# A written-out order of two blocks in turn, with one gating product in six moved from VectorE to GpSimd

## The chip, the cores and the metric

The kernel runs on one core of a Trainium2 chip. The metric is the device time of one execution in microseconds (us). Before the change the median of three runs is 351.76 us (350.42 to 352.13). A smaller time is better. Engines are named as in the profile: PE (TensorE), with PEld for its weight loads, DVE (VectorE), ACT (ScalarE), POOL (GpSimd) and SP (SyncE, which only issues transfers here).

## The reference

Two layers follow each other. The first is a causal convolution over 7 tokens with softmaxed weights per head (8 heads of 24 channels). The second multiplies a value projection by a gate and projects the product; the gate is the sigmoid of a causal per-channel convolution over 5 tokens.

```python
w = softmax(weight)                                    # (8 heads, 7 taps)
out = einsum('hk,bskhg->bshg', w, windows_of_7(x))     # x: (8, 4224, 192)
gate_pre = sum(conv_w[k] * shifted(out, k) for k in range(5))
gate = 1 / (1 + exp(-gate_pre))
val = out @ w_val                                      # 192 x 192
return (gate * val) @ w_out                            # 192 x 192
```

## The kernel before

Channels lie on partitions and tokens along the free axis. The 192 channels of a token are cut in two: 128 channels fill all partitions, and the other 64 of two halves of the batch lie above each other. So a block of m tokens (482 in most blocks, 432 and 288 in the first ones) has three parts: chunk 1, two columns groups of 128 x m (written 128x964 in the profile), and chunk 2, one of 128 x m (128x482). There are 37 blocks (0 to 36), which come from 14 groups of input; a group of the long kind holds three blocks.

For each group PE makes the first convolution as many small products with a banded matrix (`conv_unit`, L323), in units of up to 7 windows; two units belong to each block. ACT copies each half of a unit out of its bank to SBUF (`evict`, L335, tile `e`), and transfers (L381) bring it into the layout of the blocks. The five-token gate convolution is then built on DVE in two PSUM accumulators: `pa` for chunk 1 and `pb` for chunk 2. ACT opens an accumulator with the first tap (L418), DVE adds the four others (L436, a "tap"; A below stands for a tap of `pa`, B for one of `pb`), and ACT closes it with the sigmoid (L449, tile `g`).

The value projection `v` and the output projection `o` are done in split precision. An operand is cast to a rounded high part (`xh` for the input, `ph` for the gated product) and a low part, the difference (`xl`, `pl`, POOL, L458 for chunk 1 and L466 for chunk 2); three products high x high, low weight x high, high x low are summed. The cast of chunk 1 is ACT's (L457), that of `xh` of chunk 2 POOL's in most blocks and that of `ph` of chunk 2 ACT's (both L465). On PE one block has these stages: `diagonal` (L492, 64x64 products), `columns` (L540, 128x64), `rows` (L529, 64x128) and `main` (L507, 128x128), for v of block n and o of block n-1. Gating is DVE's: `gated` multiplies the bank of v by `g` in place (L558), once for chunk 2 and twice for chunk 1. ACT copies the three banks of o to SBUF (`project`, L574), and SP sends them out. In the last seven blocks chunk 2 of v is first copied from its bank by ACT (L746, tile `vt`) and multiplied on POOL (L750).

The order on every engine is the order in which the program calls these functions; a loop body from L705 on is the same for blocks 4 to 29. Five PSUM banks are handed out in rotation to v, o and the units, whichever comes next; each taker waits for whoever reads the bank's last content.

```python
    for n in range(HEAD, WHOLE):
        diagonal(n)
        taps({HEAD: "", HEAD + 1: "BBABA"}.get(n, "BABA"))
        ...
        columns("v", n)
        gated(n, 2)
        columns("o", n - 1)
        project(n - 1, 2)
        split_gated2(n)
        taps("AABAA" if n == HEAD else "ABAB")
        ...
        conv(todo[n], True)
```

Of the kernel before, what the change touches and what calls it, by code (L numbers as in the profile page):

```python
# [24 lines left out]
NS = 5  # L25
# [66 lines left out]

UNIT = {2: 4, 3: 6, 5: 7}
# [11 lines left out]
SOON = {2: (0, 0, 1, 1), 3: (1, 2, 2, 2), 4: (3, 3, 3, 4, 4, 4), 5: (5, 5, 6, 6, 7, 7)}  # L105


@with_exitstack
def kernel(
# [21 lines left out]
    ps = ctx.enter_context(tc.tile_pool(name="ps", bufs=5, space=PSUM))  # L131
# [76 lines left out]

    def zeros(k):
        pw = ps.tile([128, 512], F32, tag="p", name="pw")  # L210
        for i in range(k):
            nc.tensor.matmul(pw[:M, :ZW], lhsT=zero[:, :M], rhs=zero[:, M:], start=True, stop=True)  # L212

# [93 lines left out]
    def conv_unit(u, hold=False):  # L307
        g, q, ws = units[u]
        n = NJS[g]
        if u == first_unit[g]:  # L310
            x1s[g] = xp.tile([128, 2 * XB], F32, tag="x1", name=f"x1_{g}")
            x2s[g] = xp.tile([128, XC], F32, tag="x2", name=f"x2_{g}")
        if ws[0] == (0, 0):
            es[g, q] = ep.tile([M, 4 * NMAX * WIN], F32, tag="e", name=f"e_{g}_{q}")
        e = es[g, q]
        pc = [ps.tile([128, 512], F32, tag="p", name=f"pc_{u}_{r}") for r in range(2)]
        for k, (hi, j) in enumerate(ws):
            h = QUADS[q][hi]
            i, at = home[g, h]
            c = (at * n + j) * M  # L320
            for r, c0, c1 in ((0, 0, 64), (1, 64, M), (0, 64, M), (1, 0, 64)):
                p = HALVES[r]
                nc.tensor.matmul(  # L323
                    pc[r][c0:c1, k * HW : (k + 1) * HW],
                    lhsT=xtiles[i][p, c + c0 : c + c1],
                    rhs=band[p, 4 * q + hi, :],
                    start=True,
                    stop=True,
                )
        a = ws[0][0] * n + ws[0][1]  # L330
        w = len(ws)
        ev = e[:, : 4 * n * WIN].rearrange("p (w r t) -> p w r t", r=2, t=HW)

        def evict(r):
            nc.scalar.copy(ev[:, a : a + w, r, :], pc[r][:M, : w * HW].rearrange("p (w t) -> p w t", t=HW))  # L335

        evict(0)
        if hold:
            held.append(lambda: (evict(1), send_rows(g, q, ws, e)))
        else:  # L340
            evict(1)
            send_rows(g, q, ws, e)

    held = []

    def release():
        for f in held:
            f()
        held.clear()
# [14 lines left out]
    def scatter(g, h, e):  # L364
# [11 lines left out]
        def rows(c0, c1):  # L376
            return e[c0 * NS : c1 * NS, :]

        def send(dst, c0, c1, a, b, dma=dma):
            w = NS * (b - a)  # L380
            dma(dst[:, :w].rearrange("p (s t) -> p s t", s=NS), rows(c0, c1)[:, a:b])  # L381
# [22 lines left out]
    accs, g1s, g2s, xs, pr, ots, banks, sums = {}, {}, {}, {}, {}, {}, {}, {}  # L404
# [48 lines left out]
    def split1(pool, tag, n, x):  # L453
        m = STEPS[n][2]
        h = pool.tile([128, 2, MB], F32R, tag="h", name=f"{tag}h_{n}")[:, :, :m]
        l = pool.tile([128, 2, MB], F32R, tag="l", name=f"{tag}l_{n}")[:, :, :m]
        nc.scalar.copy(h, x)  # L457
        nc.gpsimd.tensor_tensor(out=l, in0=x, in1=h.bitcast(F32), op=ALU.subtract)  # L458
        return h, l

    def split2(pool, tag, n, x, copy=nc.scalar.copy):
        m = STEPS[n][2]
        h = pool.tile([128, MB], F32R, tag="h2", name=f"{tag}h2_{n}")[:, :m]
        l = pool.tile([128, MB], F32R, tag="l2", name=f"{tag}l2_{n}")[:, :m]
# [18 lines left out]
    def diagonal(n):  # L483

        for what, m in (("v", n), ("o", n - 1)):
            if ok(m):
                acc = bank(what, m, 2)
                w, x = (w_val, views(m)[1]) if what == "v" else (w_out, g2s[m])
                for r in range(2):
                    dst = acc[HALVES[r if what == "v" else 1 - r]]  # L490
                    w22 = w.f[HALVES[r], W22 + 64 * r : W22 + 64 * r + 64]
                    nc.tensor.matmul(dst, lhsT=w22, rhs=x[HALVES[r]], start=True, stop=False)  # L492

    def main(what, n, q):
        if not ok(n):
            return
# [14 lines left out]
    def rows(what, n):  # L511
        if not ok(n):
            return
# [11 lines left out]
        w, _, _, h2, l2 = operands(what, n)  # L525
# [7 lines left out]
    def columns(what, n):  # L533
        if not ok(n):
            return
# [6 lines left out]
    def split(n):  # L542
        if n >= PLAIN:
            return
        x1, x2 = views(n)
        if n < 2:
            xs[n, 2] = split2(sp, "x", n, x2)
        elif HEAD < n < WHOLE:
            xs[n, 2] = split2(sp, "x", n, x2, nc.gpsimd.tensor_copy)
        xs[n, 1] = split1(sp, "x", n, x1)  # L550
        if 2 <= n <= HEAD:
            xs[n, 2] = split2(sp, "x", n, x2)

    def gated(n, q):
        if not ok(n):
            return
        v = g1s[n][:, q] if q < 2 else g2s[n]
        nc.vector.tensor_tensor(out=v, in0=banks.pop(("v", n, q)), in1=v, op=ALU.mult)  # L558

    def split_gated1(n):  # L560
        if ok(n):
            pr[n, 1] = split1(pp, "p", n, g1s[n])

    def split_gated2(n):
        if ok(n) and n < WHOLE:
            pr[n, 2] = split2(pp, "p", n, g2s[n])

    def project(n, q):
        if not ok(n):
            return  # L570
# [3 lines left out]
        nc.scalar.copy(ots[n][:, q * m : (q + 1) * m], banks.pop(("o", n, q)))  # L574
# [3 lines left out]
        elif q == 1:  # L578
# [10 lines left out]
    def conv(k, hold=False):  # L589
        for i in range(k):  # L590
            if done[0] < len(units):
                conv_unit(done[0], hold and i == k - 1)
                done[0] += 1
# [22 lines left out]
    split(0)  # L616
# [12 lines left out]

    for n in range(HEAD):  # L630
        diagonal(n)
        split(n + 1)
        main("v", n, 0)
        main("v", n, 1)
        if n != 1:
            gate_taps(n + 1, 0, 1, 2)
        columns("v", n)
        gated(n, 2)
        if n:
            gate_taps(n + 1, 0, 1 if n == 1 else 2, 2 if n == 1 else 3)  # L640
        columns("o", n - 1)
        split_gated2(n)
        project(n - 1, 2)
        rows("v", n)
        gated(n, 0)
        gated(n, 1)
        rows("o", n - 1)
        main("o", n - 1, 0)
        project(n - 1, 0)
        main("o", n - 1, 1)  # L650
        project(n - 1, 1)
        conv(1)
        if n < 2:
            split_gated1(n)
        conv(todo[n] - 1)
        if n < 2:
            gate_taps(n + 1, 0, 2, 3)
            gate_taps(n + 1, 1, 1, 2)
            gate_taps(n + 1, 0, 3, 4)
            gate_taps(n + 1, 1, 2, 3)  # L660
        else:
            gate_taps(n + 1, 0, 3, 4)
            gate_taps(n + 1, 1, 1, 3)
        gate_taps(n + 1, 0, 4, 5)
        if n == HEAD - 1:
            break
        gate_close(n + 1, 0)
        gate_open(n + 2, 0)
        if n >= 2:
            split_gated1(n)  # L670
        gate_taps(n + 1, 1, 3)
        gate_close(n + 1, 1)
        gate_open(n + 2, 1)
    gate_taps(HEAD, 1, 3)
    for i in range(2):
        gate_close(HEAD, i)
    gate_open(HEAD + 1, 0)
    split_gated1(HEAD - 1)
    gate_open(HEAD + 1, 1)


    line = [
        [(n, k) for n in range(HEAD + 1, N) for k in range(2 if i and n in SUMMED else 1, KG)] for i in range(2)
    ]
    pending = []

    def taps(order):
        for c in order:
            i = "AB".index(c)
            if line[i]:  # L690
                n, k = line[i].pop(0)
                gate_taps(n, i, k, k + 1)
                if k == KG - 1:
                    pending.append((n, i))

    def close():
        for n, i in pending:
            gate_close(n, i)

    def reopen():  # L700
        for n, i in pending:
            gate_open(n + 1, i)
        pending.clear()

    for n in range(HEAD, WHOLE):  # L705
        diagonal(n)
        taps({HEAD: "", HEAD + 1: "BBABA"}.get(n, "BABA"))
        if HEAD < n <= LAST:
            split_gated1(n - 1)
        close()  # L710
        release()
        reopen()
        split(n + 1)
# [145 lines left out]
```

## Time and profile before

| What | Value |
|---|---|
| median of 3 runs | 351.76 us (350.42 to 352.13) |
| the profiled execution, its own time | 352.94 us |
| its span, first to last instruction | 350.8 us |
| PE busy | 336.4 us, 96% |
| DVE busy | 320.4 us, 91% |
| ACT busy | 311.0 us, 89% |
| POOL busy | 252.8 us, 72% |
| granted PE clock, mean | 0.992 of full speed |
| HBM, over the span | 160 GB/s |

The busy share of PE is no measure of how near it is to its limit, since the modelled ends of its products overlap the next ones; what counts there is the distance from start to start. The shares are means over the whole span. The middle, some 180 us in which one block follows another with a fixed period, has to be read by itself.

### The profile page before, as it was taken

Reading aid. Unit: us, or ns where it says so; the run is one execution under the profiler, and the core shown is the slowest. Engines: PE = TensorE matmul, PEld = TensorE weight load, DVE = VectorE, ACT = ScalarE, POOL = GpSimd, SP = SyncE. Lnnn points to the kernel's source line nnn. Section 1 sums busy time; section 2 is a strip of 40 time slices with the busy share of each in tenths; the row PEclk is TensorE's granted clock in tenths of the full one; section 3 lists DMA queues with packets and bytes.
Section 4 is the critical chain, followed back from the end, with each engine's and each line's share of the span. In section 5 each row is a group of like instructions: output and inputs, shape, how many; then the busy total and the mean of one; then the engine's idle time right before and its main releaser. Section 6 shows DMA issues by size and latency. Waiting matters only on the chain.

```text
span 350.8 us, 12959 instructions
## 1 busy us (share of the span) xinstructions
PE 336.4 (96%) x5334; PEld 210.9 (60%) x5334; DVE 320.4 (91%) x427; ACT 311.0 (89%) x544; POOL 252.8 (72%) x195
## 2 busy tenths in 40 slices
PE   8778998999999999999999999999999999999995
PEld 7756655766666666666666666666666665533343
DVE  3898988898999999999999999999999998999950
ACT  7478989787998999999999999999999999999842
POOL 1859855676877888888888888887887877755551
PEclk9999999899999999999999999999999999999998
DMA  7889879899898898898798798798898783442223
GB/s 249 268 212 277 245 235 284 228 274 287 252 277 295 244 295 258 241 277 273 227 283 277 207 286 299 208 283 290 219 293 267 202 314 120 169 152 117 85 86 130
DMA packets 38947, 83.19 MB, mean 237 GB/s; under 512 B 4936, under 2 KB 17008, under 8 KB 38888
## 3 DMA queue, kind: packets, MB, share of 16 engines
q1 hardware_dynamic: 37440, 80.64, 74.9%
q0 software_dynamic: 896, 1.27, 1.5%
q8 instruction: 42, 0.69, 0.9%
q10 hardware_dynamic: 552, 0.46, 0.5%
q14 instruction: 17, 0.14, 0.1%
HBM read 30.06 MB, written 26.00 MB: 160 GB/s over the span
## 4 chain that ended last, share of the span: by engine, by line
PE 84%; DMA 4%; ACT 3%; issue 3%; DVE 2%; SPq 2%; POOL 1%; ACTq 0%; DVEq 0%; POOLq 0%
PE o L507 14%; PE pc L323 14%; PE v L507 11%; PE v L540 9%; PE o L540 8%; PE o L529 6%; PE v L492 6%; PE v L529 5%; PE o L492 5%; DMA x<-e 3%; PE v L500 2%; PE o L521 2%; PE v L521 2%; PE pw L212 1%; DVE pa L436 1%
## 5 line engine op out<-in xcount | busy, mean ns | idle before, releaser
L436 DVE SCALAR_TENSOR_TENSOR pa<-x,cwt,pa 128x964 f32<-128x964 f32 (+4 forms) x148 | 173.4, 1172 | 5.4 <-ACT pa L418 4.9
L458 POOL TENSOR_TENSOR pl<-g,ph 128x964 fp32r<-128x964 f32 (+4 forms) x37 | 79.5, 2150 | 72.1 <-ACT ph L457 63.6
L436 DVE SCALAR_TENSOR_TENSOR pb<-x,cwt,pb 128x482 f32<-128x482 f32 (+4 forms) x142 | 98.6, 694 | 0.3
L558 DVE TENSOR_TENSOR g<-v,g 128x482 f32<-128x482 f32 (+4 forms) x105 | 63.5, 630 | 10.4 <-ACT g L449 3.9
L574 ACT COPY ot<-o 128x482 f32<-128x482 f32 (+4 forms) x111 | 59.7, 547 | 14.7 <-PE o L507 10.2
L323 PE MATMUL pc<-band,x 64*64 64x58 f32 (+1 forms) x3776 | 66.5, 220 | 5.0 <-issue 1.8
L323 PEld LDWEIGHTS pc<-band,x 64*56 64x56 f32 (+1 forms) x3776 | 60.8, 132 | 17.1 <-issue 11.0
L458 POOL TENSOR_TENSOR xl<-x,xh 128x964 fp32r<-128x964 f32 (+2 forms) x32 | 64.3, 2009 | 1.7 <-ACT xh L457 1.6
L335 ACT COPY e<-pc 120x348 f32<-120x348 f32 (+2 forms) x148 | 61.7, 473 | 3.8 <-PE pc L323 3.8
L418 ACT ACTIVATE pa<-x,cwt 128x964 f32<-128x964 f32 (+4 forms) x37 | 38.1, 1029 | 2.7 <-issue 1.6
L457 ACT CAST ph<-g 128x964 fp32r<-128x964 f32 (+4 forms) x37 | 35.8, 966 | 3.8 <-DVE g L558 3.8
L466 POOL TENSOR_TENSOR xl<-x,xh 128x482 fp32r<-128x482 f32 (+2 forms) x30 | 34.2, 1139 | 5.6 <-ACT xh L465 3.6
L449 ACT ACTIVATE g<-pa 128x964 f32<-128x964 f32 (+4 forms) x37 | 34.9, 944 | 3.7 <-DVE pa L436 3.3
L492 PE MATMUL v<-x,wvf 64*64 64x482 f32 (+4 forms) x148 | 37.5, 553 | 0.0
L540 PE MATMUL v<-x,wvf 128*64 128x482 f32 (+4 forms) x148 | 37.4, 572 | 0.0
L492 PE MATMUL o<-g,wof 64*64 64x482 f32 (+4 forms) x148 | 36.5, 567 | 0.8 <-ACT e L335 0.8
L540 PE MATMUL o<-g,wof 128*64 128x482 f32 (+4 forms) x148 | 35.5, 547 | 0.0
L466 POOL TENSOR_TENSOR pl<-g,ph 128x482 fp32r<-128x482 f32 (+2 forms) x30 | 35.2, 1172 | 0.0
L507 PE MATMUL o<-ph,woh 128*128 128x482 f32 (+4 forms) x74 | 31.3, 422 | 0.2 <-ACT ph L457 0.2
L457 ACT CAST xh<-x 128x964 fp32r<-128x964 f32 (+2 forms) x32 | 31.2, 974 | 0.0
L507 PE MATMUL o<-pl,woh 128*128 128x482 f32 (+4 forms) x74 | 27.8, 376 | 1.5 <-POOL pl L458 1.5
L507 PE MATMUL o<-ph,wol 128*128 128x482 f32 (+4 forms) x74 | 27.3, 369 | 0.0
(79 smaller groups left out, 482.8 us busy)
## 6 DMA issues: line engine op xcount, KB each, us to landing
x<-xw SPq DMA_DIRECT2D x72, 300.0 KB
out<-ot SPq DMA_DIRECT2D x27, 723.0 KB
x<-e SPq DMA_DIRECT2D x45, 271.9 KB
x<-xw SPq DMA_DIRECT2D x16, 360.0 KB
x<-e SPq DMA_DIRECT2D x36, 135.9 KB
out<-ot SPq DMA_DIRECT2D x6, 648.0 KB
x<-e SPq DMA_DIRECT2D x20, 163.1 KB
x<-e SPq DMA_DIRECT2D x18, 90.6 KB
```

The source lines that it names most:

```text
L323: nc.tensor.matmul(pc[r][c0:c1, k * HW : (k + 1) * HW], lhsT=xtiles[i][p, c + c0 : c + c1], rhs=band[p, 4 * q + hi, :], start=True, stop=True,
L335: nc.scalar.copy(ev[:, a : a + w, r, :], pc[r][:M, : w * HW].rearrange("p (w t) -> p w t", t=HW))
L436: nc.vector.scalar_tensor_tensor(out=acc, in0=views(n, k)[i], scalar=cwt[:, i, k : k + 1], in1=acc, op0=ALU.mult, op1=ALU.add,)
L457: nc.scalar.copy(h, x)
L458: nc.gpsimd.tensor_tensor(out=l, in0=x, in1=h.bitcast(F32), op=ALU.subtract)
L466: nc.gpsimd.tensor_tensor(out=l, in0=x, in1=h.bitcast(F32), op=ALU.subtract)
L492: nc.tensor.matmul(dst, lhsT=w22, rhs=x[HALVES[r]], start=True, stop=False)
L507: nc.tensor.matmul(acc, lhsT=a[:, r], rhs=b[:, q], start=(fresh and i == 0), stop=(not fresh and i == 2))
L529: nc.tensor.matmul(acc, lhsT=a[p, r], rhs=b[p], start=(fresh and i == 0), stop=(not fresh and i == 2))
L540: nc.tensor.matmul(acc[HALVES[q if what == "v" else 1 - q]], lhsT=w.f[:, W12 : W12 + 64], rhs=x[:, q], start=False, stop=True)
L558: nc.vector.tensor_tensor(out=v, in0=banks.pop(("v", n, q)), in1=v, op=ALU.mult)
L574: nc.scalar.copy(ots[n][:, q * m : (q + 1) * m], banks.pop(("o", n, q)))
```

## The change

A table `ORDER` with one line of tokens for each block replaces the loops. Each token is one call: A and B are taps, `cv`/`co` columns of v and o, `rv`/`ro` rows, `mv0`.. `mo1` mains, `dv`/`do` diagonals, `c1 c2` units, `e10`.. `e21` their evictions, `g0 g1 g2` gating, `sA oA sB oB` closing and opening the accumulators, `xh xl ph pl` casts and differences (2 for chunk 2, P for a cast on POOL), and `+1`, `-1` another block. Blocks 6 to 27 alternate between two lines, an odd and an even one:

```diff
+    dv o0-2 g1-1 ph-1 xh+1 B c1-1 e10-1 ph2P-1 pl2-1 A co-1 B e11-1 A o2-1 o1-2 B pl-1 cv c2-1 rv vt e20-1
+    e21-1 sB gp ro-1 A mv1 oB+1 A B mo1-1 mv0 sA+1 g1 oA+2 B mo0-1 ph2P pl2 xh2P+1 o1-1 c1 g0 xl+1 o0-1 do e10
+    A
...
+    dv c2-1 e11-1 co-1 B ph-1 cv e20-1 xh+1 A e21-1 A ro-1 B o2-1 xl2 sB A rv g2 pl-1 oB+1 mv0 g0 mv1 xh2P+1
+    xl+1 xl2+1 mo1-1 sA+1 oA+2 mo0-1 B do
...
-    ps = ctx.enter_context(tc.tile_pool(name="ps", bufs=5, space=PSUM))
+    ps = ctx.enter_context(tc.tile_pool(name="ps", bufs=1, space=PSUM))
...
+    free = [ps.tile([128, 512], F32, tag=f"p{i}", name=f"p_{i}") for i in range(5)]
+    def take(key):
+        taken[key] = free.pop(0)
+        return taken[key]
+
+    def give(key):
+        free.append(taken.pop(key))
...
+    def copy_v(n):
+        vts[n] = vp.tile([128, MB], F32, tag="vt", name=f"vt_{n}")[:, : STEPS[n][2]]
+        nc.scalar.copy(vts[n], drop("v", n, 2))
+
+    def gate_v(n):
+        nc.gpsimd.tensor_tensor(out=g2s[n], in0=vts.pop(n), in1=g2s[n], op=ALU.mult)
...
+    def step(t, n):
+        copy = nc.gpsimd.tensor_copy if t[-1] == "P" else nc.scalar.copy
+        t = t.removesuffix("P")
...
+        elif t == "vt":
+            copy_v(n)
+        elif t == "gp":
+            gate_v(n)
```

In the odd blocks 7 to 27 (eleven) chunk 2 is gated by `vt` on ACT and `gp` on POOL in place of DVE's `g2`; the cast `ph` of chunk 2 is POOL's in blocks 6 to 27; and a freed bank goes to the back of a list from whose front the next taker is served. Blocks 0 to 5 and 28 to 36 keep their work and nearly their order. The counts on each engine: DVE has 11 instructions fewer, ACT 12 fewer, POOL 34 more, PE and SP as many as before.

On DVE, first the rows of one block before the change (block 14; `pb`, `pa` are taps, `g_14` written from `v_` the products):

```order
L436 SCALAR_TENSOR_TENSOR pb_2553<-x_6_1861,cwt,pb_2553 128x482
L436 SCALAR_TENSOR_TENSOR pa_2605<-x_6_1860,cwt,pa_2605 128x2x482
L436 SCALAR_TENSOR_TENSOR pb_2553<-x_6_1861,cwt,pb_2553 128x482
L436 SCALAR_TENSOR_TENSOR pa_2605<-x_6_1860,cwt,pa_2605 128x2x482
L558 TENSOR_TENSOR g_14_2691<-v_2_2677,g_14_2691 128x482
L436 SCALAR_TENSOR_TENSOR pa_2605<-x_6_1860,cwt,pa_2605 128x2x482
L436 SCALAR_TENSOR_TENSOR pb_2700<-x_6_1861,cwt,pb_2700 128x482
L436 SCALAR_TENSOR_TENSOR pa_2605<-x_6_1860,cwt,pa_2605 128x2x482
L436 SCALAR_TENSOR_TENSOR pb_2700<-x_6_1861,cwt,pb_2700 128x482
L558 TENSOR_TENSOR g_14_2603<-v_0_2733,g_14_2603 128x482
L558 TENSOR_TENSOR g_14_2603<-v_1_2734,g_14_2603 128x482
```

And DVE in an odd block of the changed kernel (block 13, whose products are the two rows with `g_13`):

```order
L717 TENSOR_TENSOR g_12_2160<-p_123,g_12_2160 128x482
L615 SCALAR_TENSOR_TENSOR pb_2291<-x_5_1335,cwt,pb_2291 128x482
L615 SCALAR_TENSOR_TENSOR pa_2310<-x_6_1761,cwt,pa_2310 128x2x482
L615 SCALAR_TENSOR_TENSOR pb_2291<-x_5_1335,cwt,pb_2291 128x482
L615 SCALAR_TENSOR_TENSOR pa_2310<-x_6_1761,cwt,pa_2310 128x2x482
L615 SCALAR_TENSOR_TENSOR pb_2291<-x_5_1335,cwt,pb_2291 128x482
L615 SCALAR_TENSOR_TENSOR pa_2310<-x_6_1761,cwt,pa_2310 128x2x482 x2
L615 SCALAR_TENSOR_TENSOR pb_2436<-x_6_1762,cwt,pb_2436 128x482
L717 TENSOR_TENSOR g_13_2308<-p_122,g_13_2308 128x482
L615 SCALAR_TENSOR_TENSOR pb_2436<-x_6_1762,cwt,pb_2436 128x482
L717 TENSOR_TENSOR g_13_2308<-p_121,g_13_2308 128x482
```

The product of chunk 2 is gone from this block, and two taps of the same accumulator now stand behind each other (`x2`), which happens once in an odd and once in an even block.

On POOL, two blocks before the change (`pl` and `xl` are differences, `xh_16` the cast of the input's chunk 2):

```order
L458 TENSOR_TENSOR xl_2707<-x_6_1860,xh_2706 128x2x482
L466 TENSOR_TENSOR pl_14_2718<-g_14_2691,ph_14_2717 128x482
L458 TENSOR_TENSOR pl_2843<-g_14_2603,ph_2842 128x2x482
L465 CAST xh_16_2855<-x_6_1861 128x482
L466 TENSOR_TENSOR xl_16_2856<-x_6_1861,xh_16_2855 128x482
```

And POOL from an even block into the odd block 15 of the changed kernel:

```order
L647 TENSOR_TENSOR pl_2533<-g_13_2308,ph_2532 128x2x482
L642 CAST xh_15_2580<-x_6_1762 128x482
L647 TENSOR_TENSOR xl_2539<-x_6_1761,xh_2538 128x2x482
L647 TENSOR_TENSOR xl_15_2581<-x_6_1762,xh_15_2580 128x482
L642 CAST ph_14_2641<-g_14_2560 128x482
L647 TENSOR_TENSOR pl_14_2642<-g_14_2560,ph_14_2641 128x482
L647 TENSOR_TENSOR pl_2603<-g_14_2446,ph_2602 128x2x482
L724 TENSOR_TENSOR g_15_2705<-vt_2697,g_15_2705 128x482
L642 CAST ph_15_2737<-g_15_2705 128x482
L647 TENSOR_TENSOR pl_15_2738<-g_15_2705,ph_15_2737 128x482
```

POOL has got the two casts `ph_14` and `ph_15` and the product `g_15`, and the difference of chunk 1 of `ph` has moved behind those of chunk 2.

On PE, in the odd block 13 of the changed kernel, between `columns` (L713) and what follows:

```order
L713 MATMUL p_121<-g_12_2160,wof 64x482 x2
L713 MATMUL p_124<-x_5_1334,wvf 64x482 x2
L502 MATMUL p_125<-band,x_2131 64x58
L502 MATMUL p_123<-band,x_2131 56x58
L502 MATMUL p_125<-band,x_2131 56x58
L502 MATMUL p_123<-band,x_2131 64x58
```

A unit of the first convolution now stands between `columns` and `rows`; before the change the rows of L529 followed those of L540 directly, and both units of a block stood together at its end.

## Rows read from the trace of the kernel before

**Rows 1.** Chain that ended last, in order of time, 179 to 206 us (start, length).

```profile
181.96 1.73 PE pc L323 x102
...
190.82 1.61 PE pc L323 x95
```

**Rows 2.** Timeline of all engines, 180 to 191 us (start, length, engine, line, operation, operands).

```profile
181.14 0.98 ACT L449 ACTIVATE g<-pa 128x964 f32<-128x964 f32 x1
...
182.16 1.07 ACT L418 ACTIVATE pa<-x,cwt 128x964 f32<-128x964 f32 x1
...
183.17 1.28 ACT L335 COPY e<-pc 120x406 f32<-120x406 f32 x3
...
183.49 0.59 PE L492 MATMUL v<-x,wvf 64*64 64x482 f32 x1
...
183.71 0.62 PE L492 MATMUL o<-g,wof 64*64 64x482 f32 x2
...
184.67 1.03 PE L540 MATMUL v<-x,wvf 128*64 128x482 f32 x4
...
186.43 0.48 PE L529 MATMUL o<-ph,woh 64*128 64x482 f32 x2
...
187.94 0.49 PE L507 MATMUL o<-ph,woh 128*128 128x482 f32 x1
...
188.27 0.38 PE L507 MATMUL o<-ph,wol 128*128 128x482 f32 x1
...
188.49 0.38 PE L507 MATMUL o<-pl,woh 128*128 128x482 f32 x1
...
188.90 1.22 ACT L574 COPY ot<-o 128x482 f32<-128x482 f32 x2 [0.26 <-PE o L507]
...
190.01 0.98 ACT L449 ACTIVATE g<-pa 128x964 f32<-128x964 f32 x1
```

**Rows 3.** Timeline of DVE, 170 to 182 us.

```profile
172.54 1.25 DVE L558 TENSOR_TENSOR g<-v,g 128x482 f32<-128x482 f32 x2
173.71 0.71 DVE L436 SCALAR_TENSOR_TENSOR pb<-x,cwt,pb 128x482 f32<-128x482 f32 x1
174.39 1.23 DVE L436 SCALAR_TENSOR_TENSOR pa<-x,cwt,pa 128x964 f32<-128x964 f32 x1
175.52 0.72 DVE L436 SCALAR_TENSOR_TENSOR pb<-x,cwt,pb 128x482 f32<-128x482 f32 x1
...
177.28 0.65 DVE L558 TENSOR_TENSOR g<-v,g 128x482 f32<-128x482 f32 x1
177.85 1.22 DVE L436 SCALAR_TENSOR_TENSOR pa<-x,cwt,pa 128x964 f32<-128x964 f32 x1
```

**Rows 4.** Timeline of DVE, 292 to 345 us: three taps of one accumulator.

```profile
301.70 3.75 DVE L436 SCALAR_TENSOR_TENSOR pa<-x,cwt,pa 128x964 f32<-128x964 f32 x3
```

**Rows 5.** Timeline of POOL, 118 to 185 us.

```profile
169.82 0.60 POOL L465 CAST xh<-x 128x482 fp32r<-128x482 f32 x1
170.50 1.23 POOL L466 TENSOR_TENSOR xl<-x,xh 128x482 fp32r<-128x482 f32 x1
171.70 2.08 POOL L458 TENSOR_TENSOR xl<-x,xh 128x964 fp32r<-128x964 f32 x1
173.74 1.21 POOL L466 TENSOR_TENSOR pl<-g,ph 128x482 fp32r<-128x482 f32 x1
176.50 2.26 POOL L458 TENSOR_TENSOR pl<-g,ph 128x964 fp32r<-128x964 f32 x1 [1.55 <-ACT ph L457]
178.69 0.59 POOL L465 CAST xh<-x 128x482 fp32r<-128x482 f32 x1
```

**Rows 6.** Groups by line and shape (count | busy us, mean ns | idle before).

```profile
L465 ACT CAST ph<-g 128x482 fp32r<-128x482 f32 x22 | 13.9, 630 | 0.0
...
L750 POOL TENSOR_TENSOR g<-vt,g 128x482 f32<-128x482 f32 x5 | 6.1, 1229 | 0.0
```

**Rows 7.** Timeline of DVE, 40 to 100 us: one tap.

```profile
85.55 1.23 DVE L436 SCALAR_TENSOR_TENSOR pa<-x,cwt,pa 128x964 f32<-128x964 f32 x1 [1.60 <-ACT pa L418]
```

More of the change, by code (lines that the diff above doesn't have):

```diff
@@ L329, in conv_unit, with evict @@
                 )
+    def evict(u, r):
+        g, q, ws = units[u]
+        n = NJS[g]
         a = ws[0][0] * n + ws[0][1]
         w = len(ws)
[L332 to L341, printed above, removed]
-            send_rows(g, q, ws, e)
[L344 to L349, printed above, removed]
+        me = 64 + M - cut(g)
+        e = es[g, q]
+        ev = e[:me, : 4 * n * WIN].rearrange("p (w r t) -> p w r t", r=2, t=HW)
+        nc.scalar.copy(
+            ev[:, a : a + w, r, :], taken["c", u, r][:me, : w * HW].rearrange("p (w t) -> p w t", t=HW)
+        )
+        give(("c", u, r))
+        if r:
+            send_rows(g, q, ws, e)
     def send_rows(g, q, ws, e):
@@ L400, in views, with outs @@
         return x1v[:, :, o + k : o + k + m], x2s[g][:, o + k : o + k + m]
[L404 removed]
+    accs, g1s, g2s, xs, pr, ots, banks, sums, vts = {}, {}, {}, {}, {}, {}, {}, {}, {}
+    did = set()
+    def outs(n):
+        return [(f"o{q}", n) for q in range(3)]
     def gate_open(n, i):
@@ L481, in ok, with diagonal @@
         return 0 <= n < N
[L483 to L492, printed above, removed]
+    def diagonal(what, n):
+        acc = bank(what, n, 2)
+        w, x = (w_val, views(n)[1]) if what == "v" else (w_out, g2s[n])
+        for r in range(2):
+            dst = acc[HALVES[r if what == "v" else 1 - r]]
+            w22 = w.f[HALVES[r], W22 + 64 * r : W22 + 64 * r + 64]
+            nc.tensor.matmul(dst, lhsT=w22, rhs=x[HALVES[r]], start=True, stop=False)
     def main(what, n, q):
-        if not ok(n):
-            return
         fresh = (what, n, q) not in banks
@@ L587, with conv @@
     done = [0]
[L589 to L593, printed above, removed]
+    def conv(k):
+        for u in range(done[0], min(done[0] + k, len(units))):
+            conv_unit(u)
+            for r in range(2):
+                evict(u, r)
+            done[0] += 1
     todo = [0] * (N + 1)
@@ L628 @@
     gate_open(1, 1)
[L630 to L713, printed above, removed]
-        columns("v", n)
-        gated(n, 2)
-        columns("o", n - 1)
-        project(n - 1, 2)
-        split_gated2(n)
-        taps("AABAA" if n == HEAD else "ABAB")
-        def outputs():
-            for q in range(2):
-                main("o", n - 1, q)
-                project(n - 1, q)
-        rows("o", n - 1)
-        rows("v", n)
-        outputs()
-        close()
-        reopen()
-        for q in range(2):
-            main("v", n, q)
-            gated(n, q)
-        conv(todo[n], True)
@@ L781, with tap, evicts @@
-    assert not held
+    unit_of = {}
+    u = done[0]
+    for n in range(N):
+        unit_of[n] = list(range(u, min(u + todo[n], len(units))))
+        u += len(unit_of[n])
+    assert u == len(units)
+    line = {
+        c: [(n, k) for n in range(1, N) for k in range(2 if i and n in SUMMED else 1, KG)]
+        for i, c in enumerate("AB")
+    }
+    def tap(c):
+        if line[c]:
+            n, k = line[c].pop(0)
+            gate_taps(n, "AB".index(c), k, k + 1)
+    def evicts(n, i, r):
+        if i <= len(unit_of[n]):
+            evict(unit_of[n][i - 1], r)
```

340 lines of the change are left out of this document (238 added, 102 removed).

## The prediction

> **What bounds the kernel now.** I first read the chain of work that ended last. From about 100 to 285 us it is PE's and repeats with each block: units, diagonals, columns, rows, mains. Two blocks later the same piece stands again: a unit stretch begins at 181.96 and the next at 190.82 us, a period of 8.86 us [rows 1], so 17.72 us for a pair of blocks. The two stretches differ (1.73 and 1.61 us, 14 and 13 windows), while the period stays; PE is therefore not simply full, and something closes a loop.
>
> The timeline shows the loop. ACT closes `pa` at 181.14, opens the next at 182.16 and only then, at 183.17, copies the first half unit out of its bank. PE's diagonal of v starts at 183.49, but that of o, which takes this very bank, at 183.71, when the copy (about 0.5 us of the 1.28 for three) is done. From there PE runs through: columns at 184.67, rows at 186.43, mains at 187.94, and ACT's copy of the first output, which waited 0.26 us for PE, starts at 188.90; two copies later, at 190.01, ACT closes `pa` again [rows 2]. The reader should see that the steps 1.02 + 1.01 + 0.54 + 0.96 + 1.76 + 1.51 + 0.96 + 1.11 add up to 8.87: the loop between PE and ACT is the period.
>
> DVE comes out almost the same. From start to start an A tap followed by B takes 1.13 us (174.39 to 175.52), B and A together 1.76 (175.52 to 177.28), so B 0.63; a product followed by a tap takes 0.57, and two products in a row 1.17 [rows 3]. A block is 4 A + 4 B + 3 products = 4.52 + 2.52 + 1.74 = 8.78 us, 0.08 under the period; the B after the two products takes 0.68 in place of 0.63, since the A behind it waits for ACT's opening. So two limits lie on each other, and a gain on DVE alone is worth at most 0.08 per block unless the loop of PE and ACT opens too. POOL needs 0.68 + 1.20 + 2.04 + 1.21 + 2.19 = 7.32 us in a block and waits 1.55 for ACT's cast `ph` [rows 5].
>
> **The change, part by part,** for a pair of blocks.
>
> DVE loses one product of six. Its cost there is 0.57 to 0.585 [rows 3]. But the pair has two places with A directly behind A. Three such taps took 3.75 us, which is 1.22 + 2 x 1.265 [rows 4]: each costs 0.135 more than an A behind a B. New sum: 8 x 1.13 + 8 x 0.63 + 5 x 0.575 + 0.27 = 17.22, against 17.56. So 0.34 us, not 0.58.
>
> POOL gets two casts `ph` and a product. The product has a row of its own from the last blocks, 1.23 us [rows 6]; the cast of `ph` on POOL has none for this shape, and I take the cast of `xh`, 0.68 to the start of its successor (bounds: its own 0.59, and 1.2 if it cost as much as a two-operand difference of that size) [rows 5]. Sum 2 x 7.32 + 2 x 0.68 + 1.23 = 17.23 (17.0 to 18.3). It was 14.64 of 17.72 with room; now it is as full as DVE.
>
> ACT loses two casts of 0.63 [rows 6] and gains a copy like that of an output, some 0.56 (1.11 for two [rows 2]): 0.7 less. It waited 0.26 per block for PE [rows 2], so it gets room and drops out as a limit.
>
> PE's work is the same; what counts is the loop. In the new order the diagonal of o stands behind a unit, and takes a bank that ACT copied out much earlier, not the one just filled; so the wait at 183.71 goes. Without it PE needs 8.86 less the 0.1 to 0.3 us that the diagonal of o stood (0.22 from v's start at 183.49 to 183.71, of which some 0.1 is issue) [rows 2], about 8.65, or 17.3 for a pair. Against that stands the unit that now lies between columns and rows of each odd block: one more change of the shape of PE's products. What such a change costs, the rows show at the mains: the first one after rows takes 0.33 us to its successor (187.94 to 188.27), the next 0.22 [rows 2], so 0.11 a change; bounds nothing, if the unit hides its own loads, and 0.38, if the whole length of such a product has to run out. PE's sum: 17.4 (17.2 to 17.8).
>
> [...]
>
> The largest sum before was 17.56, and the pair took 17.72. Now three engines stand at 17.2 to 17.4 and no wait of a full loop is left; I take 17.45 for the pair, 0.27 less. Pairs that count: blocks 8 to 27, ten of them. In blocks 6 and 7 DVE waited 1.60 us for an accumulator whose opening hangs on data that arrive late [rows 7], so what DVE saves there is not saved. Blocks 0 to 5 and 28 to 36 keep their work. Sum 10 x 0.27 = 2.7 us: 352.94 of the profiled execution becomes 350.2, and as the median of the runs is 1.18 lower, 351.76 becomes 349.0.
>
> The hand-out of banks costs nothing by itself: a bank freed first is taken first, and the takers that I followed find theirs copied out before PE comes to them. Its cover is ACT's new room of about 0.6 a pair; where that is used up, PE stands at `ro` in the odd block, which needs the bank of the eviction just ahead, and 0.1 there is 1 us in ten pairs.
>
> **Rivals.** *DVE sets the pace.* If PE's extra change costs nothing, the pair takes DVE's 17.22 to 17.25: 10 x 0.48 = 4.8 us less, 347.0. For it: DVE runs without a gap in the old period. Against it: PE and POOL would have to be late nowhere.
>
> *PE loses it in its changes of shape.* With 0.38 for the extra one the pair takes 17.7: no change, 351.8. For it: every first product after a change is longer [rows 2]. Against it: the excess there was 0.11.
>
> *POOL becomes the bound; this one ends slower.* Its 17.23 hold no wait at all, and today it stands 1.55 us in each block until ACT has cast `ph` [rows 5]. In the new order the product `gp` waits for ACT's sigmoid and `vt` as well. One such wait left in each pair gives 18.78, 10 x 1.06 = 10.6 us more: 362. It decides from 0.49 us of waiting a pair on; the time passes 0.5% from 0.67 on. For it: POOL's order is strict, and rows of v and o need its differences. Against it: the difference that waits now stands behind a cast and a difference of chunk 2, 1.9 us that need nothing from ACT.
>
> *Data come late.* Evictions of the second unit of a block stand a block later than before. If an opening then waits as at 85.55 [rows 7], 1.6 us in each of seven groups, the time is 363. Against it: in the middle DVE waits for no opening longer than 0.05, so there is room.
>
> **How the numbers follow.** Chances: the forecast 0.42, DVE's pace 0.18, PE's changes 0.20, POOL 0.13, late data 0.07. Half a percent, 1.76 us, is about what a measurement of this kernel can tell from no change. The forecast's own bounds, 0.13 to 0.40 a pair, are 347.8 to 350.5, and a seventh of it lies within 0.5%. So faster 0.36 + 0.18 = 0.54 (0.55), same 0.06 + 0.20 = 0.26 (0.25), slower 0.20. The range leaves out the two slow cases: from DVE's pace with a little over, 346.6, to PE's with the spread of the runs, 352.8.
>
> **What would show it.** In the profile after: two blocks in 17.45 us between equal pieces of the chain between 100 and 270 us; DVE's busy time 6 to 7 us less (eleven products), still without gaps there; POOL nearly full, over 17 us of each pair, with waits under 0.5; ACT with idle stretches of 0.3 to 0.6 us ahead of its closings; PE's diagonal of o no longer behind an eviction; and the first row product after a unit at 0.3 to 0.4 us. Wrong would be: POOL without gaps and DVE waiting for PE's products, which means POOL; DVE with gaps ahead of A, which means ACT or data; equal periods with PE's stages stretched at their first products, which means the changes of shape.

## The result and the profile after

The changed kernel takes 356.55 us (median of 4 executions, 354.79 to 360.88) beside 351.59 for the kernel before (4, 350.42 to 352.13): ratio 1.0129, 95% interval 1.0080 to 1.0178. It is slower, clear of the spread. Side by side on two other chips the ratio was 1.0066 (1.0019 to 1.0114) and 1.0048 (1.0018 to 1.0078), so the loss is less there, about half a percent. The prediction said 349.0. The ratios, here and below, leave out executions over 1.5% above the fastest of their kernel, so they need not be the quotient of the medians beside them.

In the code after, taps stand at L615, openings at L597, closings at L628, products at L717 and, on POOL, L724, casts at L642, differences at L647, evictions at L518, scatters at L556; on PE units are L502, diagonals L671, columns L713, rows L704 and mains L684. All banks are called `p`.

The engines' busy time from the page of the changed kernel:

```profile
PE 334.7 (94%) x5334; PEld 215.1 (61%) x5334; DVE 315.4 (89%) x416; ACT 306.8 (86%) x532; POOL 277.8 (78%) x229
```

And its busy time in a window, 120 to 200 us (length; PE, PEld, DVE, ACT and POOL in us with their instructions in brackets; granted clock, share of the DMA engines, GB/s):

```profile
120.00:200.00 80.00, 80.00 (x1377) 53.38 (x1378) 78.92 (x97) 75.76 (x125) 75.78 (x61) 1.00 0.88 260
```

POOL's share went from 72 to 78% of the span; in the middle it is busy 75.78 of 80 us, DVE 78.92. The chain that ended last has the same piece, columns of v and o, twice a pair there:

```profile
114.44 1.77 PE p L713 x8
...
131.91 1.77 PE p L713 x8
...
149.29 1.77 PE p L713 x8
...
166.92 1.77 PE p L713 x8
...
184.40 1.77 PE p L713 x8
...
201.78 1.77 PE p L713 x8
```

Five pairs take 87.34 us, 17.47 each; before it was 17.72 [rows 1]. So the middle does what the prediction said. The loss is elsewhere, and the starts of ACT's closings of `pa`, block by block, show where. At block 22 the changed kernel is still ahead: its closing starts at 214.59, that of before at 216.57. Three steps from one closing to the next stand out in it, and a fourth, 16 to 17, in other runs (in us; the first two rows are the two kernels, the others are runs told below):

| kernel | block 7 to 8 | 16 to 17 | 22 to 23 | 28 to 29 |
|---|---|---|---|---|
| before | 9.99 | 8.81 | 8.84 | 8.81 |
| changed | 12.07 | 8.56 | 12.26 | 12.07 |
| the same again | 14.02 | 8.98 | 8.64 | 10.42 |
| the same, a third time | 12.29 | 8.60 | 9.12 | 12.95 |
| half the zeros' width | 9.11 | 10.38 | 10.49 | 10.72 |
| less output | 8.45 | 8.56 | 8.55 | 12.27 |
| late outputs and 40 instructions | 10.73 | 8.56 | 8.55 | 10.45 |

The step from 22 to 23, in the timeline of the changed kernel:

```profile
211.45 1.04 PE L502 MATMUL p<-band,x 64*64 64x58 f32 x56
...
214.87 0.48 PE L704 MATMUL p<-xh,wvh 64*128 64x482 f32 x2 [2.38 <-ACT pb L597]
...
215.38 0.48 PE L704 MATMUL p<-xl,wvh 64*128 64x482 f32 x2
...
215.60 0.66 PE L704 MATMUL p<-ph,woh 64*128 64x482 f32 x2
...
216.00 0.67 PE L704 MATMUL p<-ph,wol 64*128 64x482 f32 x2
...
216.78 1.07 ACT L597 ACTIVATE pa<-x,cwt 128x964 f32<-128x964 f32 x1 [1.22 <-DMA x<-e]
...
218.68 0.66 DVE L717 TENSOR_TENSOR g<-p,g 128x482 f32<-128x482 f32 x1 [3.31 <-PE p L684]
```

The same piece a pair earlier:

```profile
194.89 0.49 PE L704 MATMUL p<-xh,wvh 64*128 64x482 f32 x2
195.22 0.38 PE L704 MATMUL p<-xh,wvl 64*128 64x482 f32 x2
195.44 0.38 PE L704 MATMUL p<-xl,wvh 64*128 64x482 f32 x2
...
196.42 0.67 ACT L597 ACTIVATE pb<-x,cwt 128x482 f32<-128x482 f32 x1
```

Two things meet in the step from 22 to 23. PE ends a unit and stands 2.38 us. ACT's opening of `pb`, which the row names, is only what happened last: a pair earlier the same row products began at 194.89, at once behind their unit, 1.5 us before ACT came to that opening (196.42). And ACT's opening of `pa` for block 23 waits 1.22 us for transferred data.

### The profile page after: what moved, and what is told of

It is laid out like the page before. It is cut to its first block, busy times and chain, and to the rows that moved or that the text cites. A ratio compares the mean times of both kernels' runs of the same rounds, so it can differ in the third digit from the quotient of the medians.

```text
span 354.9 us, 12961 instructions
## 1 busy us (share of the span) xinstructions
PE 334.7 (94%) x5334; PEld 215.1 (61%) x5334; DVE 315.4 (89%) x416; ACT 306.8 (86%) x532; POOL 277.8 (78%) x229
## 4 chain that ended last, share of the span: by engine, by line
PE 77%; ACT 6%; DVE 5%; DMA 5%; SPq 2%; issue 2%; DVEq 0%; ACTq 0%
PE p L684 23%; PE p L713 16%; PE p L502 13%; PE p L704 11%; PE p L671 8%; DMA x<-e 4%; PE p L696 4%; DVE pa L615 3%; PE p L677 2%; ACT pa L597 2%; SPq L556 2%; ACT g L628 2%; ACT e L518 2%; PE p L390 1%; DVE pb L615 1%
## 5 line engine op out<-in xcount | busy, mean ns | idle before, releaser
L615 DVE SCALAR_TENSOR_TENSOR pa<-x,cwt,pa 128x964 f32<-128x964 f32 (+4 forms) x148 | 173.2, 1170 | 8.0 <-ACT pa L597 5.2
L647 POOL TENSOR_TENSOR pl<-g,ph 128x482 fp32r<-128x482 f32 (+4 forms) x67 | 114.2, 1711 | 39.7 <-ACT ph L642 33.1
L647 POOL TENSOR_TENSOR xl<-x,xh 128x964 fp32r<-128x964 f32 (+5 forms) x62 | 96.8, 1583 | 6.9 <-ACT xh L642 6.5
L615 DVE SCALAR_TENSOR_TENSOR pb<-x,cwt,pb 128x482 f32<-128x482 f32 (+4 forms) x142 | 98.4, 693 | 2.9 <-ACT pb L597 2.2
L502 PEld LDWEIGHTS p<-band,x 64*56 64x56 f32 (+1 forms) x3776 | 65.1, 132 | 39.0 <-ACT ot L730 13.0
L502 PE MATMUL p<-band,x 64*56 64x58 f32 (+1 forms) x3776 | 71.3, 219 | 11.0 <-issue 3.5
L717 DVE TENSOR_TENSOR g<-p,g 128x482 f32<-128x482 f32 (+4 forms) x94 | 57.5, 625 | 14.9 <-PE p L684 7.0
L730 ACT COPY ot<-p 128x482 f32<-128x482 f32 (+4 forms) x111 | 57.1, 547 | 13.2 <-PE p L684 10.5
L518 ACT COPY e<-p 120x348 f32<-120x348 f32 (+2 forms) x148 | 63.2, 477 | 6.0 <-PE p L502 5.1
L597 ACT ACTIVATE pa<-x,cwt 128x964 f32<-128x964 f32 (+4 forms) x37 | 38.1, 1029 | 5.5 <-DMA x<-e 4.0
L642 ACT CAST ph<-g 128x964 fp32r<-128x964 f32 (+7 forms) x44 | 39.0, 887 | 3.8 <-DVE g L717 3.8
L628 ACT ACTIVATE g<-pa 128x964 f32<-128x964 f32 (+4 forms) x37 | 34.6, 934 | 5.5 <-DVE pa L615 4.9
L671 PE MATMUL p<-x,wvf 64*64 64x482 f32 (+4 forms) x148 | 37.4, 560 | 0.0
L671 PE MATMUL p<-g,wof 64*64 64x482 f32 (+4 forms) x148 | 36.8, 561 | 0.0
L713 PE MATMUL p<-g,wof 128*64 128x482 f32 (+4 forms) x148 | 36.6, 573 | 0.0
L713 PE MATMUL p<-x,wvf 128*64 128x482 f32 (+4 forms) x148 | 36.2, 568 | 0.0
L642 ACT CAST xh<-x 128x964 fp32r<-128x964 f32 (+4 forms) x37 | 33.0, 905 | 0.0
L724 POOL TENSOR_TENSOR g<-vt,g 128x482 f32<-128x482 f32 (+2 forms) x17 | 20.9, 1227 | 11.9 <-ACT g L628 11.9
L684 PE MATMUL p<-ph,woh 128*128 128x482 f32 (+4 forms) x74 | 29.2, 394 | 0.0
L684 PE MATMUL p<-ph,wol 128*128 128x482 f32 (+4 forms) x74 | 27.5, 372 | 0.0
L684 PE MATMUL p<-pl,woh 128*128 128x482 f32 (+4 forms) x74 | 27.5, 371 | 0.0
L684 PE MATMUL p<-xh,wvh 128*128 128x482 f32 (+2 forms) x64 | 26.7, 418 | 0.0
```

Source lines behind the costliest of these rows:

```text
L502: nc.tensor.matmul(pc[r][64 * s : 64 * s + c1 - c0, k * HW : (k + 1) * HW], lhsT=xtiles[i][p, c + c0 : c + c1], rhs=band[p, 4 * q + hi, :] ...
L518: nc.scalar.copy(ev[:, a : a + w, r, :], taken["c", u, r][:me, : w * HW].rearrange("p (w t) -> p w t", t=HW))
L597: nc.scalar.mul(acc, views(n, 0)[i], cwt[:, i, 0:1])
L615: nc.vector.scalar_tensor_tensor(out=acc, in0=views(n, k)[i], scalar=cwt[:, i, k : k + 1], in1=acc, op0=ALU.mult, op1=ALU.add,)
L628: nc.scalar.activation(dst, accs.pop((n, i)), AF.Sigmoid)
L642: copy(two[0], x)
```

## The experiments

**What is chance.** The kernel unchanged.

> The changed kernel once more, nothing edited. In its first trace three steps from one closing of `pa` to the next took 12.1 to 12.3 us in place of 8.4 to 9.1: in blocks 7, 22 and 28. If each belongs to a fixed place in the program, the same three steps are long again (block 22 by 3 us or more) and the time is 355 to 358. If the one in block 22, where PE stood 2.4 us behind a unit with nothing named that it waited for, is chance, it is absent here or stands elsewhere, and a trace without it has a span of about 351.5.

355.03 us (10 executions, 352.25 to 359.96) beside 354.59: 1.0066. The step in block 22 was 8.64, so PE's stand is not a fixture. The wait at block 8 was longer, 3.24 us (table). What is fixed is where things can go wrong, not whether they do.

**PE's program, moved.** Does PE's stand of 2.4 us in block 21 keep its block when only its place in PE's program moves?

```diff
-        for i in range(k):
-            nc.tensor.matmul(pw[:M, :ZW], lhsT=zero[:, :M], rhs=zero[:, M:], start=True, stop=True)
+        for i in range(2 * k):
+            nc.tensor.matmul(pw[:M, : ZW // 2], lhsT=zero[:, :M], rhs=zero[:, M : M + ZW // 2], start=True, stop=True)
```

> The 30 products with zeros that PE does ahead of its data become 60 of half the width, so all that follows stands some 120 PE instructions later in PE's program, and no order is changed. [...] Theory of late data or of a wait between engines: same block, same 2.4 us, 356.5.

361.16 us, 1.0236 (1.0162 to 1.0310). The doubled products cost 4.7 us before the first closing (26.07 in place of 21.37), so the time tells nothing; the trace does. PE's stand was gone from block 21, and there was one in block 3, inside a unit, and a shorter one in block 6, between columns; and openings of `pa`, six blocks apart, waited for data:

```profile
61.75 0.50 PE L502 MATMUL p<-band,x 64*56 64x58 f32 x18 [2.29 <-issue]
...
85.30 0.58 PE L713 MATMUL p<-g,wof 128*64 128x432 f32 x2 [0.65 <-issue]
...
171.08 1.07 ACT L597 ACTIVATE pa<-x,cwt 128x964 f32<-128x964 f32 x1 [2.18 <-DMA x<-e]
...
225.51 1.07 ACT L597 ACTIVATE pa<-x,cwt 128x964 f32<-128x964 f32 x1 [2.29 <-DMA x<-e]
```

So there are two causes, not one.

**The hand-out of banks alone.** `ONE` is the line of block 28, `FIVE` that of block 5 without its last two tokens.

```diff
+ORDER = ORDER[:5] + (FIVE,) + (ONE,) * 22 + ORDER[28:]
```

> The table holds the order of before in blocks 5 to 28; what is left of the change is the hand-out of banks as they become free. If that costs nothing, 351 to 352.5 and a period of 8.86 us a block. If the hand-out itself makes PE wait for banks, 354 or more, with stands of PE ahead of diagonals or units that before did not have.

354.91 us beside 354.59, 1.0052 (1.0005 to 1.0100), on a chip where both spread from 349.8 to 358. The trace decides: from the closing of block 10 to that of block 28 it takes 159.50 us, before 159.48, and PE stands nowhere that it did not before. The hand-out costs nothing in the middle, and the old order from the table with two edits more, told below, stands at 1.0003 of before.

**A later entry.**

```diff
+ORDER = ORDER[:5] + (FIVE,) + (ONE,) * 5 + (ONE + "do A",) + (ORDER[6],) + ORDER[13:]
```

> The pairs begin with block 12 in place of block 6, eight pairs in place of eleven. Theory of the entry: at block 6 the new order puts two units off and gains about 2 us by it, loses them to an opening that waits for data until 83.63 us, and pays for the two units when it is left in block 27 (3.3 us). From block 12 on no opening waits, so the 2 us are kept: before less 8 x 0.25, plus 3.3 less 2.0, is about 351, and up to 354.5 if PE's single stand comes too. Rival: entering and leaving cost the same wherever they are; then 356.

354.04 us, 1.0029 (0.9984 to 1.0075), within the first expectation's 354.5 for a trace in which PE stands too, and not its 351. Block 8's opening waited 1.88 us although the old order still ran there: that wait belongs to the head of either kernel. From block 12 on the trace has the two causes again, in blocks 15, 21 and 27 PE's:

```profile
161.13 0.49 PE L708 MATMUL p<-xh,wvl 64*128 64x482 f32 x2 [1.21 <-issue]
...
215.08 0.49 PE L708 MATMUL p<-ph,woh 64*128 64x482 f32 x2 [1.01 <-issue]
...
268.96 0.49 PE L708 MATMUL p<-pl,woh 64*128 64x482 f32 x2 [0.83 <-issue]
```

They come every six blocks, each two kinds of row products later in the program than the last.

**Less to transfer.** Only a ninth of each block's output is written, in both kernels:

```diff
-            nc.sync.dma_start(out[:, o : o + 3 * m], ots[n][:, : 3 * m])
+            nc.sync.dma_start(out[:, o : o + m // 3], ots[n][:, : m // 3])
```

> The changed kernel, but each block's transfer of the output carries a ninth of its columns (all but the last block); the rest of the output is left out. Theory of late data: in the changed kernel 7 to 9 us lie between the issue of a group's last transfer and the opening that reads it (10 to 11.6 before), and a transfer lands after up to 8; with some 0.65 MB less to move a block it lands earlier, so the waits of ACT's openings in blocks 8, 17, 23 and 29 go, PE's stands without a named cause too, a pair stays at 17.4 to 17.5, and the span is about 347. Rival, that the long steps come from the order itself (banks, engines): they stay, and the time is above 353.

> The kernel before with the same part of the output left out, as the other side of the comparison. Its openings wait for data only near 84 us, so it loses that wait of 1.6 us and keeps its period of 8.86: about 350, and 2 to 3 us more than the changed kernel with the same part left out. If the lighter traffic speeds it up by as much as the changed kernel, late data are not what the change added.

348.65 us (347.87 to 350.48) and 349.50 (348.75 to 351.32), beside 352.24 for the kernel before. With little output the changed order is no slower, 0.85 us ahead. No opening from block 11 on waits, and nine pairs from closing 10 to 28 take 156.79, 17.42 each. Two expectations failed. PE still stood 1.47 us in block 27, so light traffic alone does not end its stands. And the two kernels are 0.85 us apart, not 2 to 3: the lighter traffic takes 2.7 us off the kernel before, too. The changed kernel was not run on this chip; by its ratios elsewhere (1.0048, 1.0066) it would take some 354 there, an estimate, so that the lighter traffic is worth 5 to 6 us to it.

**Outputs sent later.** An output that is ready is issued on SP behind the next eviction that ends a second unit.

```diff
-            nc.sync.dma_start(out[:, o : o + 3 * m], ots[n][:, : 3 * m])
+            late.append((out[:, o : o + 3 * m], ots[n][:, : 3 * m]))
+            if not 6 <= n < 26:
+                flush()
...
             evict(unit_of[n][i - 1], r)
+            if (i, r) == (2, 1):
+                flush()
```

> The changed kernel with all its work; in blocks 6 to 25 the transfer of a finished output is issued only behind the next eviction that ends a block's second unit, so up to two of these transfers (723 KB each) no longer go ahead of a group's last transfers of input. Theory of late data: these land some 2 to 4 us earlier, the waits at the openings of blocks 17 and 23 fall under 0.3 us, and the time is 350 to 353. Rival: the waits stay, 355 or more.

> The changed kernel with late outputs once more, with more executions. Expected 0.3 to 0.6% under the kernel before, no wait over 0.3 us of an opening in blocks 11 to 29. If its first result was chance, within 0.2% of before.

350.35 us (10 executions, 348.70 to 355.43) beside 352.24, ratio 0.9953 (0.9913 to 0.9993), then 352.67 (12, 348.08 to 357.05) beside 352.37, ratio 0.9936 (0.9893 to 0.9979). In both traces the openings of blocks 11 to 29 wait no more, as expected. But the executions fall into two groups, about 350 and about 354, and PE still stands without a named cause, in the first trace in blocks 8 and 9, in the second in block 9:

```profile
104.13 0.38 PE L684 MATMUL p<-xh,wvl 128*128 128x482 f32 x1 [0.95 <-issue]
...
110.69 0.34 PE L502 MATMUL p<-band,x 64*64 64x58 f32 x8 [0.40 <-issue]
```

```profile
108.27 0.48 PE L504 MATMUL p<-band,x 64*64 64x58 f32 x8 [2.38 <-issue]
```

So this mends one cause only. The upper group can be the kernel's own stands, so by itself I can't call it faster.

**The product back on DVE.** First where POOL's stood, then one tap later.

```diff
-    ... vt e20-1 e21-1 sB gp ro-1 A mv1 ...
+    ... e20-1 e21-1 sB g2 ro-1 A mv1 ...
```

> The changed order with the sixth product of a pair back on DVE (no copy of v on ACT, no product on POOL). If DVE's sum of 17.22 a pair was near the limit, as predicted, it is now 17.8 and a pair takes 17.8 in place of 17.47: 3.5 us more over eleven pairs. If PE alone sets the pair at 17.4, a pair stays at 17.5 and the move of the product was worth nothing.

378.33 us: my edit put the product directly behind a closing for which DVE then waits; a pair takes 19.5 to 20, which tells nothing of DVE's sum.

> The sixth product back on DVE again, now one tap later, so that DVE does not stand until ACT has closed `pb`. DVE's sum for a pair is 17.22 + 0.575 - 0.135 (the product parts two taps of `pa`) = 17.66. If DVE is a limit nearly as near as PE, pairs go from 17.45 to about 17.7 and what the order gained in the middle is gone; if not, they stay under 17.5. Pairs above 18 would mean that DVE still stands behind the closing.

366.87 us. Eight pairs from closing 12 to 28 take 147.88, 18.49 each, and DVE has this in each:

```profile
185.69 1.22 DVE L619 SCALAR_TENSOR_TENSOR pa<-x,cwt,pa 128x964 f32<-128x964 f32 x1
187.43 0.66 DVE L721 TENSOR_TENSOR g<-p,g 128x482 f32<-128x482 f32 x1 [0.53 <-issue]
```

DVE still stands there 0.53 us, behind the closing; with the work of 17.66 that was reckoned for it that is 18.2 of the 18.5. So DVE seems to pace this kernel, but not by its work alone, and how long a pair would be without that stand was not tried. In the two places that were tried the product on DVE costs the pair 1 to 2.5 us.

**Forty instructions.** Ten short products with zeros more, ahead of the data.

```diff
     zeros(WARM[2])
+    pw = take("pw")
+    for i in range(10):
+        nc.tensor.matmul(pw[:M, :4], lhsT=zero[:, :M], rhs=zero[:, M : M + 4], start=True, stop=True)
+    give("pw")
```

> Ten very short products with zeros more ahead of PE's data: PE's program behind them stands 40 instructions later, at almost no time. [...] A wait of the row products for an engine would stay at the rows.

351.58 us (350.11 to 354.30), 0.9987 (0.9946 to 1.0027). No PE stand without a named cause over 0.3 us from 60 us on, neither in the units nor at the rows: the old places are empty, and no new one was seen. Data still came late: the opening of block 23 waited 1.39 us.

**Side by side on one chip.** The changed kernel, the 40 instructions, late outputs with them, and both with the pairs from block 8:

> The changed kernel once more, on the same chip and in turn with the three kernels that follow. Both theories: about 353 to 356, with executions far apart.

> The changed kernel with PE's program 40 instructions later. [...] If data alone were the cause, no difference over 0.5 us.

> Late outputs and the 40 instructions together. [...]

> The same with pairs from block 8 on. Theory of the entry: within 1 us of the kernel with both, since one pair less (0.27) stands against an entry that loses less to data; 349 to 350.5, with executions nearer together.

| kernel | median (12 executions each) | ratio to before (352.12), 95% |
|---|---|---|
| changed | 353.92 (351.86 to 361.25) | 1.0048 (1.0018 to 1.0078) |
| 40 instructions | 352.24 (349.11 to 354.95) | 0.9993 (0.9963 to 1.0022) |
| and late outputs | 350.60 (347.51 to 353.50) | 0.9944 (0.9917 to 0.9971) |
| and pairs from block 8 | 350.46 (348.83 to 352.27) | 0.9956 (0.9933 to 0.9978) |

By the medians each edit is worth about 1.7 us; the intervals of neighbouring rows overlap a little, so each share is rough, while both edits together stand clear of the changed kernel. In the trace with the 40 instructions alone the opening of block 23 waited 1.88 us and PE stood nowhere without a named cause. In the trace with both, nine pairs from closing 10 to 28 take 156.87, 17.43 each, and no step there is over 9.13. The place of entry makes no difference that shows. Before that, late outputs with pairs from block 8, without the 40 instructions:

> Outputs sent behind evictions as in the kernel with late outputs, and the pairs begin with block 8 in place of 6, behind the opening of block 8 that waits for data in nearly every trace. Theory: what the new order gains by putting two units off (1.5 to 2 us) is kept, since no opening waits behind it; ten pairs at 0.27; leaving costs 1.6. So 1.9 less + 2.7 less + 1.6 more is 3.0 less than before, about 349. If the place of entry does not matter, it stands within 0.7 us of the late outputs alone.

351.35 us (350.02 to 353.25), 0.9973 (0.9943 to 1.0003); PE stood in block 27, by 1.22 us, and the last long step was 11.94. That is 2.3 us above the expectation.

**Is it the order?** The old order with the two edits, and the new one once more:

> The order of before (from the table, banks handed out as free) with the late outputs and the 40 instructions. In the old order no opening in the middle waits and PE never stands without a named cause, so neither should bring anything: 351 to 353, within 0.3% of before. If it is faster by 0.4% or more, the gain of the kernel with both is not the new order's.

> The new order with late outputs and the 40 instructions once more, beside it: 0.4 to 0.7% under before, 349.5 to 350.7. If it is chance, no difference from the old order with the same two edits.

352.81 us, 1.0003 (0.9973 to 1.0032), and 350.67, 0.9943 (0.9908 to 0.9977), beside 352.96. The two edits do nothing for the old order. The new order with both edits is 0.6% under the kernel before and under the old order with the same edits. By the forecast it was to be 0.8% under.

## Why the prediction was wrong

**The middle was right.** A pair was forecast at 17.45 (17.72 before); it takes 17.47 in the changed kernel's trace and 17.42 to 17.43 where nothing is late. That the figure is met to 0.03 is partly luck, since it was chosen between PE's 17.4, with bounds of 17.2 and 17.8, and the other sums. The first row product behind a unit takes 0.33 to its successor, the next 0.22 (194.89, 195.22 and 195.44): the 0.11 for a change of shape is measured again, not the 0.38 of a product run out. ACT stands for PE's mains ahead of a copy of the output, 0.28 to 0.50 us a pair, and at most 0.22 ahead of a closing, where the prediction had looked for 0.3 to 0.6; in the window PE is busy throughout, which fits PE setting the pair. POOL's product waits 0.33 to 0.78 for ACT's closing (126.40 to 196.47). I had put the point from which POOL decides at 0.49, and pairs with 0.77 or 0.78 take 17.38 to 17.63 between the columns, those with 0.33 and 0.43 take 17.47 and 17.48: POOL's sum of 17.23 was too large, since busy 75.78 of 80 us it works 16.5 of 17.47. DVE's busy time fell by 5.0 us, not 6 to 7; it has gaps of 0.2 in which it waits for PE (136.20), so its work alone does not set the pair.

**The hand-out of banks** costs nothing, as said (159.50 against 159.48).

**The step that failed is the rival "Data come late"**: "Against it: in the middle DVE waits for no opening longer than 0.05, so there is room." That nobody waits says that there is room, not how much, and I did not measure it against what the change takes away. It can be read. The last transfer of a group on SP and the opening of `pa` that reads it, group of block 23, kernel before:

```profile
205.39 1.14 SPq L381 DMA_DIRECT2D x<-e  x1
...
217.59 1.07 ACT L418 ACTIVATE pa<-x,cwt 128x964 f32<-128x964 f32 x1
```

From the end of the issue to the opening are 11.06 us; over the groups of blocks 11 to 29 it is 10.4 to 11.6. The changed kernel:

```profile
207.25 0.80 SPq L556 DMA_DIRECT2D x<-e  x1
```

Here the opening waited until 216.78, 8.73 us; over the groups it is 7.0 to 8.7, and the longest of these are the ones that waited. "Evictions of the second unit of a block stand a block later" was in the prediction; that they take 3 to 4 us of 11 was not. The chance of 0.07 rested on this sentence. The size of "1.6 us in each of seven groups" was too large: only the groups of blocks 17, 23 and 29 waited (11 too in two traces), by nothing to 2.3 us.

**Not in the prediction at all: PE's stands without a named cause.** Its sum has no term for them. From 60 us on, the traces of the new order hold 17 stands of over 0.3 us without a named cause, the one at 214.87 among them. Counted in PE's products from the start of the kernel, they lie at few places: behind 1736 products (104.13, 0.95 us), 1864 (108.27, 2.38; 110.69, 0.40; 111.58 in the run with the product on DVE, 1.74), 2750 (0.62, same run), 3632 (214.87, 2.38) and 4515 (0.67 in the changed kernel, 1.28 in its third trace, 1.47 with less output); where the table differs, up to 7 products further. These places are one or seven steps of 126 to 128 products apart, which is 252 to 256 instructions with each product's load of weights. Six blocks are 880 products, seven steps 882 to 886: so a place comes back in every sixth block, and drifts. In the run with half the zeros' width all work stands 60 products later in the program, but the two stands (61.75 and 85.30) are behind 1105 and 1485, five and two steps of 125.5 to 126 ahead of 1736. And of the eleven traces of the new order without the 40 instructions ten have such a stand, of the five with them none. So in these traces the stands go by PE's count of instructions, not by blocks or data.

The profile lists a DMA queue of the kind "instruction". In the changed kernel its packets come one at a time, and from 61 to 295.5 us the 30 gaps between them hold 7664 instructions of PE and its loads, 255 on average. Its row for 211.75 to 212.00 us (packets, MB, share of 16 engines):

```profile
q8 instruction: 1, 0.02, 31.0%
```

That is 0.31 x 16 x 0.25 = 1.24 us for this packet; PE goes on at 214.87, 3.0 us behind its start. In each of the 17 stands PE goes on 2.2 to 3.0 us behind the start of the last packet; where a stand has a named cause, that time is anything from 0 to 10 us. In block 27 the packet began 0.2 us ahead of the second unit in the changed kernel and 0.3 behind its start with less output, and PE stood; it began 2.0 us ahead in the second trace of the changed kernel and 2.7 in the first with late outputs, and PE did not. So the steps between the places of the stands, 252 to 256 instructions, and the mean gap between these packets, 255, nearly agree. That PE waits for the packet is not shown, since no run held one back. Why the packet began 2 us later in some executions stays open, and so does why the old order, with the same units and as many instructions, never stood there.

**Entering and leaving.** The prediction gave blocks 6, 7 and 28 no price. The table's line of block 27 holds four units, that of block 6 none: two units are put off at the entry and paid for at the end. Where nothing was late, the last step takes 10.45 in place of 8.81, 1.64 more; at the entry, closing 5 to 10 took 42.22 with less output beside 43.60 for the old order with less output, 1.38 less, of which some 0.27 is the first pair's. Together half a microsecond more. But the entry's gain is lost where block 8's opening waits for data, as it does in most traces, before's too (ACT waits 1.57 there, with no cause named, and 2.52 for data in the changed kernel's).

**The sum for the profiled execution.** It took 356.72, the forecast for it was 350.2: 6.5 us. From the closings: block 22 to 23 is 3.7 us over its usual 8.55; the other steps from 10 to 28 are 157.5 where nine pairs of 17.45 are 157.05, 0.5; 28 to 29 is 3.3 over before's 8.81, 1.64 of it for the two units and the rest where PE stood 0.67. (That stand costs 1.0 from start to start: from the first row product, 268.71, to the first main, 271.26, it is 2.55 us, and 1.52 in the trace with late outputs and 40 instructions. From that main to the next columns, with units and diagonals between, it is 6.35 in place of 5.79, the other 0.6.) At block 10 the kernel was 0.63 ahead of before, where one pair of forecast gain is 0.27, so 0.4 better; and from the last closing to the end the two kernels differ by 3.78 in place of 4.35, 0.6 better. 3.7 + 0.5 + 3.3 - 0.4 - 0.6 = 6.5.

## What to carry to other kernels

That nobody waits for a transfer says nothing of the room: measure from the last issue to the reader, and take from it what an order puts off, before calling it hidden. A change that gives 0.3 us in each of ten pairs is lost by one stand of 3 us, so look for what happens once in six blocks as well as for the period. Where an engine stands without a named cause, count its instructions up to the stand, and put a few idle ones ahead of the loop: here the places of the stands were one or seven steps of 252 to 256 instructions apart, and of five traces with 40 more instructions ahead of the loop none had a stand.

## What the hardware showed unexpectedly

PE had run without a gap (22.49 of the 22.49 us from 190.00 to 212.49, at a granted clock of 1.00); after its stand of 2.38 us, and three kinds of products later, its granted clock fell. The windows view of the changed kernel around it, columns as above:

```profile
210.00:215.00 5.00, 2.62 (x66) 1.36 (x64) 4.82 (x6) 4.97 (x11) 4.23 (x3) 1.00 0.83 230
215.00:220.00 5.00, 5.00 (x22) 3.97 (x23) 1.66 (x3) 2.13 (x3) 4.86 (x6) 0.66 0.85 283
220.00:230.00 10.00, 10.00 (x156) 6.30 (x154) 9.57 (x13) 8.29 (x15) 7.42 (x6) 1.00 0.80 180
```

Products that follow each other in 0.22 us (215.38 to 215.60) then take 0.40 (215.60 to 216.00). The seven steps from 215.60 to 218.77 take 3.17 at a granted clock of 0.50; the same seven a pair earlier, from 195.66 to 197.40, took 1.74 at 1.00. The first and last rows of the seven steps a pair earlier, and the last here:

```profile
195.66 0.40 PE L704 MATMUL p<-ph,woh 64*128 64x482 f32 x2
...
197.40 0.38 PE L684 MATMUL p<-ph,wol 128*128 128x482 f32 x1
...
218.77 0.48 PE L684 MATMUL p<-ph,wol 128*128 128x482 f32 x1
```

So the slow stretch behind this stand took 1.4 us on top of the stand's length.
